# Batch 0's last slots turn their weights through VectorE and a scratch, and the last product is split into two tiles

## The chip, the cores and the metric

The kernel runs on one core of a Trainium2 chip. The metric is the device time of one execution in microseconds (us). The profile has one execution recorded by the hardware profiler; its span is the time from its first to its last instruction. All numbers are fp32.

## What is computed

Attention with a threshold for 8 batches of 8 heads, 576 rows and head size 64; then a feed-forward block with a layer norm over the 512 features, added to its own input. The reference, cut:

```python
scores = scale * np.matmul(q, k.transpose(0, 1, 3, 2))
thresh = np.max(scores, axis=-1, keepdims=True) - tau
scores = np.where(scores >= thresh, scores, -1000000000.0)
attn = np.exp(scores - np.max(scores, axis=-1, keepdims=True))
attn = attn / (np.sum(attn, axis=-1, keepdims=True) + 1e-09)
x = np.matmul(attn, v)            # heads side by side: (8, 576, 512)
...
xn = (x - mu) / np.sqrt(var + 1e-06) * g_ln
ch = np.maximum(xn @ w_ch1, 0.0) @ w_ch2     # w_ch1 512 x 2048, w_ch2 2048 x 512
return x + ch
```

The weights w_ch1 and w_ch2 arrive as 64-bit floats, and the chip converts them.

## The kernel before, in words

**Slots.** A batch is worked off in nine slots (SLOTS), numbered here n = 0, 1, ... through all batches. Slots 0 to 3 of a batch take the first 256 rows of a pair of heads, slot 4 (HP) the 64 rows left over of all pairs, and slots 5 to 8 the next 256 rows of each pair. Within a slot: TensorE makes the scores (L421) into PSUM; VectorE takes the row maxima (L435); ScalarE the exponentials into a room e (L449); VectorE masks by the threshold and sums (L456). A following slot may write its scores only when that mask has read the last ones. TensorE then multiplies the weights, turned, with v (L604, L614), one slot later.

**Two ways to turn the weights.** The product with v wants the weights transposed, in tiles em and er. Up to slot 8 (batch 0) turn_weights does it on TensorE: each block is multiplied with a diagonal matrix that holds 1/sum (L470 on ScalarE), into PSUM tiles tp and tr, and ScalarE copies these into em and er (L506, L529). From slot 9 on, turn_blocks does it: POOL divides by the sums (L472), VectorE transposes 32x32 blocks into et (L546), SyncE writes et to a scratch in DRAM (L551) and, in the next slot, fetches em and er from there (L560, L565), so that the rest of the transposition is in the addresses. by_blocks (L352) chooses. Batch 0 has its keys in another order of rows than the batches behind it (L121), so its scratch would be addressed otherwise.

**The feed-forward block.** A group is half a batch's rows (288 tokens), 16 groups in all. first_part makes the hidden layer (tile p, evicted by ScalarE, L801). Group 0 then goes through second_plain (p2, evicted at L840); the others through second_quarters, a product of quarters in seven segments of 64 matmul records each, whose sums VectorE and POOL make (L900, L908). Generators yield after each product; second_part(n, i) issues so many of these steps in each of the four quarters i of slot n that the next group is met in time. The step counts come from fixed lists (ROOM, STEPS, ready), and each engine executes its instructions in the order in which the program issues them.

**The weights' conversion.** Class Weights cuts the weights into 32 chunks of 128x512 (16 of w_ch1, 16 of w_ch2; chunk 31 is the last). A chunk is loaded from DRAM (fetch, L255, on SyncE, 512 KB), begun (two VectorE operations, L274 and L278, and two on ScalarE, L284 and L287), carried (POOL, L299), masked (VectorE, L308) and, for w_ch1, scaled (POOL, L320). Loading and conversion need room, so free lends pieces of memory that isn't in use yet: parts of w2, of hidden, of et, of x_room, of stage. fetch takes a chunk only while more than two pieces are free. BEGUN says, slot by slot, how many chunks are to be begun at three points of a slot; by slot 9 it is 32. In slots 6 to 8 six chunks a slot are begun.

**The order in a slot** (loop from L1062): scores; maxima; exponentials; quarter 0 (with the fetch of em and er, and a fetch of up to three chunks, L1077); turns of the next q and k; masks of chunks and beginning of two; quarter 1; weights (threshold, sums); masks and two more chunks; quarter 2; turn_weights or turn_blocks (L1114); a fetch of up to three chunks (L1136); masks; quarter 3; two more chunks begun. All of the loads, the scratch's write and fetch and most stores stand on SyncE's queue in this order.

**The end.** In the last group (g = 15) the last segment's product of s4 and b22 goes into one PSUM bank, is scaled by times_root (L878), added into y12, transposed (L722) and stored (L732).

Of the kernel before, what the change touches and what calls it, by code (L numbers as in the profile page):

```python
# [18 lines left out]
def kernel(  # L19
# [158 lines left out]
    class Weights:  # L178
# [13 lines left out]
        def __init__(self):  # L192
            self.chunks = [
                (w1_sb[i][:, c : c + WC], w_ch1[i * 128 : (i + 1) * 128, c : c + WC], i)
                for c in range(0, DF, WC)
                for i in range(NK)
            ] + [
                (
                    w2_sb[:, m, d : d + 4].rearrange("p d c -> p (d c)"),
                    w_ch2[d * 128 : (d + 4) * 128, m * 128 : (m + 1) * 128].rearrange(  # L200
                        "(d p) c -> p d c", p=128
                    ),
                    None,
                )
                for m in range(NK)
                for d in range(0, ND, 4)
            ]
            self.n1 = NK * (DF // WC)
            self.fetched = self.begun = self.carried = self.masked = self.scaled = 0
            self.raw, self.made, self.ticks, self.on_scalar = {}, {}, 2, []  # L210
            flat = lambda t: t.rearrange("p a b -> p (a b)")

            x_room = ffn.tile([128, NK, TOK], F32, tag="x", bufs=3, name="x_room")
            stage = self.stage = consts.tile([128, 8, WC], F32, name="stage")
            et = att.tile([128, NB, 128], F32, tag="et", bufs=1, name="et0")

            n1 = self.n1  # L220
            self.free = []
            for t, n, before in (
                (w2_sb.rearrange("p m d c -> p (m d) c"), ND // 2, lambda p: n1 + 2 * p),
                (hidden, 4, lambda p: 10),
                (et, 2, lambda p: 2 * n1),
                (x_room, 1, lambda p: 2 * n1),
                (stage, 4, lambda p: 2 * n1),
            ):
                for p in range(n):
                    self.free.append((before(p), -1, flat(t)[:, p * 2 * WC : (p + 1) * 2 * WC]))  # L230

        def piece(self, i, wait):

# [115 lines left out]
            while self.scaled < min(self.masked, self.n1):  # L349
                self.scale()  # L350

    def by_blocks(u):  # L352

        return units[u][0] > 0

    def turn(u):

        q_in, k_in = loaded.pop(u)
        qT = att.tile([128, 2, QH], F32, tag="qT", bufs=4, name="qT")
        kT = att.tile([128, S], F32, tag="kT", bufs=4, name="kT")
        ql = q_last[u % HP]
        for at in (slice(0, 8), slice(8, NB)) if u == 0 else (slice(0, NB),):
            nc.gpsimd.tensor_scalar(
                out=q_in[:, at], in0=q_in[:, at], scalar1=scl_sb, scalar2=1.0,
                op0=ALU.mult, op1=ALU.mult,  # L370
            )
        nc.vector.transpose(kT, k_in.rearrange("p n c -> p (n c)"))
        for s in range(2):
            part = q_in[:, 9 * s : 9 * s + 8]
            if by_blocks(u):
                nc.vector.transpose(
                    qT[:, s].rearrange("p (j a c) -> p a j c", j=2, a=4),
                    part.rearrange("p (a j) c -> p a j c", j=2),
                )
            else:  # L380
                nc.vector.transpose(qT[:, s], part.rearrange("p n c -> p (n c)"))
        nc.vector.transpose(
            ql.rearrange("p (t c) -> p t c", t=2),
            q_in.rearrange("p (t n) c -> p t n c", t=2)[:, :, 8],
        )
        turned[u] = (qT, kT, ql)
# [40 lines left out]
    def exponentials(n):  # L427


        neg = small.tile([128, 4], F32, tag="neg", name="neg")  # L430
        thr = small.tile([128, 4], F32, tag="thr", name="thr")
        es = e_room[(n + 1) % 2 if n < SLOTS else 0]
        for h in range(2):
            i = slice(2 * h, 2 * h + 2)
            nc.vector.tensor_reduce(  # L435
                out=neg[:, i], in_=pairs[h],
                axis=AXL.X, op=ALU.max, negate=True,
            )
            nc.gpsimd.tensor_scalar(  # L439
                out=thr[:, i], in0=neg[:, i], scalar1=-1.0, scalar2=low_sb,  # L440
                op0=ALU.mult, op1=ALU.add,
            )
            if h == 0:
                run(n, "copy")
                conversion.scale_all()
        for i in range(4):
            if i == 2:
                yield es, thr
            nc.scalar.activation(es[:, i], blocks[i], func=AF.Exp, bias=neg[:, i : i + 1])  # L449
# [82 lines left out]
            )  # L532
        yield em, er

    def turn_blocks(s, es):


        et = att.tile([128, NB, 128], F32, tag="et", bufs=1, name="et")
# [5 lines left out]
        else:  # L544
            for h in range(2):
# [2 lines left out]
                    es[:, 2 * h : 2 * h + 2].rearrange("p j (n c) -> p j n c", c=32),  # L548
                )
        scr = dram.tile([4, S, 128], F32, tag="scr", name="scr")  # L550
        nc.sync.dma_start(  # L551
            out=scr.rearrange("a (r n) x -> (a r) (n x)", r=32),
            in_=et.rearrange("p n x -> p (n x)"),
        )
        return scr

    def fetch(s, scr):

        em, er = turned_tiles(s)
        nc.sync.dma_start(  # L560
            out=em.rearrange("p a c x -> p a (c x)"),
            in_=scr[:, : J * 128].rearrange("a (p c) x -> p a (c x)", c=J),
        )
        for j in range(2):
            nc.sync.dma_start(  # L565
                out=er[64 * j : 64 * j + 64],
                in_=scr[2 * j : 2 * j + 2, J * 128 :].rearrange("a p x -> p a x"),
            )
        return em, er
# [155 lines left out]
    def send(g, m, ot):  # L725
        b, t = divmod(g, 2)
        for i in range(4):
            f = m * 128 + 32 * i
            eng = nc.sync
            if g == NG - 1:  # L730
                eng = (nc.sync, nc.gpsimd)[m % 2] if m >= HM else (nc.sync, nc.scalar)[i % 2]
            eng.dma_start(  # L732
                out=out[b, t * TOK : (t + 1) * TOK, f : f + 32].rearrange(
                    "(n r) c -> r n c", r=32
# [109 lines left out]
    def second_quarters(g, rb):  # L844
# [28 lines left out]
                at = (slice(None), slice(d, d + 4))  # L873
                eng.tensor_tensor(out=out[at], in0=in0[at], in1=in1[at], op=op)  # L874

        def times_root(out, bank):
            r = rb[:, late].unsqueeze(1).to_broadcast([128, HM, HT])
            dve.tensor_tensor(out=out, in0=bank, in1=r, op=ALU.mult)  # L878

        def segment(weights, rhs, out=None, as_it_is=False):  # L880
            bank = ps_ff.tile([128, HM, HT], F32, tag="ff", name="seg")
            for d in range(HD):
                for m in range(HM):
# [6 lines left out]
                        yield 2, 0.5  # L890
            if out is None:
                out = ffn.tile([128, HM, HT], F32, tag="part", bufs=4, name="part")
            if as_it_is:
                times_root(out, bank)
            else:
                nc.scalar.copy(out, bank)  # L896
            return out

        def add(eng, out, a, b):
            eng.tensor_tensor(out=out, in0=a, in1=b, op=ALU.add)  # L900

        def finish(eng, i, j=None):
# [6 lines left out]
            add(eng, z, z, x)  # L909

        dve, pool = nc.vector, nc.gpsimd
        done_by = pool if g < NG - 1 else dve
        later(("t3", 3, by_fours, pool, b12, b22, b12, ALU.subtract), urgent=pool)
        banks_taken[0] = True
        yield from segment(w2[0, 0], b11, y11)
# [6 lines left out]
        yield 2, 0.5  # L922
        p7 = yield from segment(s3, b12)
        yield 2, 0.5
        yield from segment(s2, b11, y21)
        need("t4")
        later(("t1", 3, by_fours, dve, b11, b22, b11, ALU.subtract), urgent=dve)
        later(
            ("u2", 1, add, pool, y21, y21, y11), ("11", 1, add, pool, y11, y11, p2),
            ("done11", 2, finish, pool, 0, 0),  # L930
        )
        yield 2, 0.5
        p4 = yield from segment(w2[1, 1], b21)
        yield 2, 0.5
        need("t1", "u2", "11")
        p5 = yield from segment(w2[1, 0], b11)
        later(
            ("u4", 1, add, dve, y12, y21, p5), ("u3", 1, add, dve, y21, y21, p7),
            ("22", 1, add, dve, y22, y21, p5), ("21", 1, add, dve, y21, y21, p4),
            ("hi", 3, finish, done_by, 1),  # L940
        )
        ends_here = g == NG - 1
        if ends_here:
            later(("done12", 2, finish, dve, 0, 1))
            later(*((f"o{m}", 1, store, dve, g, m, y[:, m]) for m in (2, 3)))
        yield 2, 0.5
        last = segment(s4, b22, as_it_is=ends_here)
        for _ in range(12):
            yield next(last)
        banks_taken[0] = False  # L950
        while waiting_mean:
            mean_of(waiting_mean.pop(0))
        p3 = yield from last
        later(("12", 1, add, dve, y12, y12, p3))
        if not ends_here:
            later(("done12", 2, finish, done_by, 0, 1))
        later(
            *((f"o{m}", 1, store, dve, g, m, y[:, m]) for m in ((2, 3, 0, 1) if g < NG - 1 else (0, 1)))
        )
        yield 2, 0.5  # L960

    def ffn_steps(g):
# [99 lines left out]
    for n in range(NS):  # L1062
# [5 lines left out]
        scores(b, s)  # L1068
        run(n, -2)
        run(n, -1)  # L1070
        rest = exponentials(n)
        es, thr = next(rest)
        run(n, 0)
# [25 lines left out]
        second_part(n, 1)  # L1099
        conversion.carry_all()  # L1100
        conversion.scale_all()
        blocks_go = by_blocks(b * HP)
        diags = weights(es, thr, blocks_go)
        run_all(aside)
        drip()
# [6 lines left out]
        conversion.carry_all()  # L1112
        box = []
        if blocks_go:  # L1114
            scr = turn_blocks(s, es)
            at_quarter(n + 1, 0, lambda s=s, scr=scr, box=box: box.append(fetch(s, scr)))
        else:

            made = turn_weights(s, es, diags)
            for i, at in enumerate(  # L1120
                (-1, -1, 0, 0) if s <= HP + 1 else (-1, -1, -1, -1) if s < 2 * HP else (-1, 0, 1, 2)
            ):
                if i < 3:
                    at_quarter(n + 1, at, next, made)
# [64 lines left out]
```

## Time and profile before

| what | us |
|---|---|
| median of 3 runs (lowest to highest) | 1357.76 (1357.47 to 1358.55) |
| the profiled execution's own time | 1357.61 |
| its span | 1355.8 |
| matmuls into tp in slots 7, 8, 9 (weights of 6, 7, 8) | 3.75, 3.75, 4.33 |
| the same into tr | 0.64, 0.64, 0.66 |
| one transpose into et (L546, 128x1152), mean | 1.374 |
| one division on POOL (L472), mean | 0.780 |
| scratch write (1152 KB), median from issue to landing | 4.9 |
| em fetch (1024 KB), the same | 5.7 |
| load of a weight chunk (512 KB), shortest, median, longest | 3.4, 4.9, 9.7 |
| last matmul's end | 1346.33 |

A line of an engine's timeline has start, length, engine, line of the kernel, operation, tile written <- tiles read, shape and count, and, in brackets, how long the engine idled before it and what it waited for. "DVE" is VectorE, "ACT" ScalarE, "PE" TensorE, "PEld" its weight loads, "SPq" SyncE's queue. Lines on matmuls often have L101, which is the helper product; there the tile tells which they are. In a table of windows a line has the window, its length, and for each engine the busy time and, in brackets, the instructions; at the end stand the clock, the DMA engines' share and GB/s.

### The profile page before, as it was taken

How to read it: one execution, taken by the hardware profiler on the slowest of the kernel's cores; microseconds unless marked ns; L12 is line 12 of the kernel's file. 1: busy time of each engine (PE TensorE's matmuls, PEld its weight loads, DVE VectorE, ACT ScalarE, POOL GpSimd, SP SyncE). 2: the span in 40 equal slices, each digit the busy share in tenths (PEclk: the TensorE clock that was granted, in tenths of full speed). 3: DMA queues.
4: the chain of work that ended last, by engine and by line, in shares of the span. 5: the costliest groups of instructions: out<-in, count | busy, mean ns of one | idle time of the engine just before them, and what ended most of it. 6: DMA issues, size and time to landing. Idle time of an engine off the chain costs nothing.

```text
span 1355.8 us, 40852 instructions
## 1 busy us (share of the span) xinstructions
PE 1326.8 (98%) x17616; PEld 1003.3 (74%) x17616; DVE 874.0 (64%) x1531; ACT 470.0 (35%) x1022; POOL 615.3 (45%) x824
## 2 busy tenths in 40 slices
PE   8999999999999999999999999999999999999997
PEld 6766657869687786968778696877869687786967
DVE  7978777666755676666766667556766667665202
ACT  4877432332423323232333323233232323333120
POOL 3554455445444344444534454443444445344312
PEclk9999999999999999999999999999999999999999
DMA  9813464457644775447744576446754376443211
GB/s 172 264 52 98 122 182 148 177 159 183 190 141 142 194 197 167 150 136 183 195 149 151 150 191 180 147 146 188 201 169 150 131 189 178 144 155 131 64 19 19
DMA packets 320996, 206.88 MB, mean 153 GB/s; under 512 B 246896, under 2 KB 278384, under 8 KB 312752
## 3 DMA queue, kind: packets, MB, share of 16 engines
q1 hardware_dynamic: 314704, 203.38, 52.0%
q8 instruction: 138, 2.26, 0.7%
q10 hardware_dynamic: 5952, 0.74, 0.4%
q0 software_dynamic: 160, 0.15, 0.1%
q14 instruction: 42, 0.34, 0.1%
HBM read 120.46 MB, written 83.76 MB: 151 GB/s over the span
## 4 chain that ended last, share of the span: by engine, by line
PE 90%; DVE 3%; ACT 2%; DMA 1%; POOL 1%; issue 1%; SPq 1%; POOLq 0%; DVEq 0%; ACTq 0%
PE p L101 37%; PE seg L101 30%; PE sc L421 10%; PE sc L604 8%; PE sc L614 2%; PE tp L101 1%; ACT e L449 1%; DVE e L456 1%; PE var L101 1%; PE mean L101 1%; SPq L118 0%; DMA x_room<-in_moe_w_ch_dram 0%; ACT em L506 0%; DMA qk_room<-in_q_dram 0%; DVE w L308 0%
## 5 line engine op out<-in xcount | busy, mean ns | idle before, releaser
L101 PE MATMUL p<-xc,w 128*64 128x288 f32 x4096 | 517.4, 408 | 6.8 <-ACT part L896 4.6
L101 PEld LDWEIGHTS p<-xc,w 128*64 128x64 f32 x4096 | 287.4, 137 | 214.4 <-issue 13.5
L435 DVE TENSOR_REDUCE neg<-sc 128x2 f32<-128x1152 f32 x144 | 188.6, 1351 | 280.8 <-PE sc L421 280.2
L472 POOL TENSOR_SCALAR e<-e,den 128x576 f32<-128x576 f32 x252 | 193.6, 780 | 133.5 <-DVE den L461 133.5
L101 PE MATMUL seg<-hidden,w 128*64 128x144 f32 x3840 | 247.9, 287 | 0.0
L101 PEld LDWEIGHTS seg<-hidden,w 128*64 128x64 f32 x3840 | 234.9, 137 | 11.5 <-issue 8.5
L456 DVE SCALAR_TENSOR_TENSOR e<-sc,thr,e 128x576 f32<-128x576 f32 x288 | 221.8, 809 | 16.9 <-POOL thr L439 11.2
L801 ACT ACTIVATE hidden<-p 128x288 f32<-128x288 f32 x256 | 106.6, 417 | 303.6 <-PE p L101 303.6
L439 POOL TENSOR_SCALAR thr<-neg,low_sb 128x2 f32<-128x2 f32 x144 | 41.4, 288 | 374.4 <-DVE neg L435 374.0
L449 ACT ACTIVATE e<-sc,neg 128x576 f32<-128x576 f32 x288 | 197.9, 755 | 2.4 <-DVE neg L435 2.4
L546 DVE STREAM_TRANSPOSE et<-e 128x1152 f32<-128x1152 f32 x112 | 153.4, 1374 | 14.7 <-POOL e L472 14.2
L421 PE MATMUL sc<-kT,qT 64*64 64x384 f32 (+3 forms) x2048 | 139.4, 403 | 3.2 <-DVE e L456 2.2
L604 PE MATMUL sc<-em,v_in 128*64 128x128 f32 (+1 forms) x2368 | 129.4, 263 | 0.0
L604 PEld LDWEIGHTS sc<-em,v_in 128*64 128x64 f32 x2368 | 122.8, 137 | 7.9
L101 PE MATMUL seg<-hidden,stage 128*64 128x144 f32 x1920 | 123.3, 286 | 0.0
L101 PEld LDWEIGHTS seg<-hidden,stage 128*64 128x64 f32 x1920 | 117.6, 137 | 2.9 <-issue 2.9
L627 ACT COPY x<-sc 128x128 f32<-128x128 f32 x120 | 31.7, 266 | 238.8 <-PE sc L421 170.4
L421 PEld LDWEIGHTS sc<-kT,qT 64*64 64x64 f32 x2048 | 76.1, 133 | 44.1 <-issue 21.2
L874 POOL TENSOR_TENSOR hidden<-hidden 128x576 f32<-128x576 f32 x60 | 84.8, 1426 | 52.1 <-ACT hidden L801 42.4
L896 ACT COPY part<-seg 128x288 f32<-128x288 f32 x74 | 29.9, 404 | 190.4 <-PE seg L101 190.0
L874 DVE TENSOR_TENSOR hidden<-hidden 128x576 f32<-128x576 f32 x60 | 51.3, 889 | 51.5 <-PE seg L101 48.5
L101 PE MATMUL seg<-hidden,e 128*64 128x144 f32 x960 | 65.3, 286 | 0.0
(145 smaller groups left out, 1098.9 us busy)
## 6 DMA issues: line engine op xcount, KB each, us to landing
scr<-et SPq DMA_DIRECT2D x63, 1152.0 KB, 4.9
em<-scr SPq DMA_DIRECT2D x63, 1024.0 KB, 5.7
q_in<-in_q_dram SPq DMA_DIRECT2D x124, 72.0 KB, 2.7
out_dram<-ot SPq DMA_DIRECT2D x248, 36.0 KB, 3.8
k_in<-in_k_dram SPq DMA_DIRECT2D x120, 72.0 KB, 3.0
er<-scr SPq DMA_DIRECT2D x126, 64.0 KB, 5.2
v_in<-in_v_dram SPq DMA_DIRECT2D x28, 256.0 KB, 5.5
w<-in_moe_w_ch_dram SPq DMA_DIRECT2D x12, 512.0 KB, 4.8
```

The source lines that it names most:

```text
L101: nc.tensor.matmul(out[r], lhsT=lhsT[:, r], rhs=rhs, **flags)
L421: nc.tensor.matmul(sc[h][64 * i : 64 * i + 64, at : at + n], lhsT=ql[r] if s == HP else qT[r, half, j * 128 + 64 * i : j * 128 + 64 * i + 64],
L435: nc.vector.tensor_reduce(out=neg[:, i], in_=pairs[h], axis=AXL.X, op=ALU.max, negate=True,)
L439: nc.gpsimd.tensor_scalar(out=thr[:, i], in0=neg[:, i], scalar1=-1.0, scalar2=low_sb, op0=ALU.mult, op1=ALU.add,)
L449: nc.scalar.activation(es[:, i], blocks[i], func=AF.Exp, bias=neg[:, i : i + 1])
L456: nc.vector.scalar_tensor_tensor(out=es[:, i], in0=blocks[i], scalar=thr[:, i : i + 1], in1=es[:, i], op0=ALU.is_ge, op1=ALU.mult, accum_o ...
L472: nc.gpsimd.tensor_scalar(out=es[:, i], in0=es[:, i], scalar1=den[:, i : i + 1], scalar2=1.0, op0=ALU.mult, op1=ALU.mult,)
L546: nc.vector.transpose(et[:, :, 64 * h : 64 * h + 64].rearrange("p n (j c) -> p j n c", j=2), es[:, 2 * h : 2 * h + 2].rearrange("p j (n c) ...
L604: nc.tensor.matmul(dst[64 * h : 64 * h + 64], lhsT=vt[:, h, c, :], rhs=pick(em[:, 2 * j : 2 * j + 2, c], h), start=c == 0 and first, stop= ...
L627: nc.scalar.copy(x_of(2 * b + (s > HP))[:, s % (HP + 1), 128 * j : 128 * j + 128], pv[j])
L801: nc.scalar.activation(hidden[:, d], p1, func=AF.Relu)
L874: eng.tensor_tensor(out=out[at], in0=in0[at], in1=in1[at], op=op)
```

## The change

- by_blocks now asks for the slot and not the batch: from FIRST = HP + 2 = 6 on the weights are turned by blocks. So slots 6, 7 and 8 change, all of batch 0. Its scratch is written in four DMAs and em fetched in four, with rows of 512 bytes.
- et is no longer lent as two pieces to the conversion. In its place the room e[1] is lent (take) from slot 7 on, when its weights (slot 6) are turned; so the exponentials from slot 7 on go into e[0].
- In second_quarters the sums u3 and 21 are made after the fifth product and not after the sixth, with other tiles of y as room; in the last group row 21 is finished there as well, then 22 and 12 behind the sixth.
- In the last group the last product is made by last_tiles as two PSUM tiles, one for each block of 128 features. Each is scaled, added, transposed and sent by itself; what is waiting is issued before the first one.

```diff
-            et = att.tile([128, NB, 128], F32, tag="et", bufs=1, name="et0")
...
-                (et, 2, lambda p: 2 * n1),
...
+        def take(self, t):
+            t = t.rearrange("p a b -> p (a b)")
+            for p in range(2):
+                self.free.append((2 * self.n1, -1, t[:, p * 2 * WC : (p + 1) * 2 * WC]))
...
-    def by_blocks(u):
-        return units[u][0] > 0
+    FIRST = HP + 2
+    def by_blocks(n):
+        return n >= FIRST
...
-            if by_blocks(u):
+            if by_blocks(units[u][0] * SLOTS + units[u][1] + (HP + 1 if s else 0)):
...
-        es = e_room[(n + 1) % 2 if n < SLOTS else 0]
+        es = e_room[(n + 1) % 2 if n <= FIRST else 0]
...
-    def turn_blocks(s, es):
+    def turn_blocks(b, s, es):
...
+        if b == 0:
+            for a in range(4):
+                nc.sync.dma_start(
+                    out=scr[a].rearrange("(n r) x -> r n x", r=32), in_=et[32 * a : 32 * a + 32]
+                )
+            return scr
...
+        for a in range(0 if b else 4):
+            nc.sync.dma_start(
+                out=em[:, a], in_=scr[a, : J * 128].rearrange("(c p) x -> p c x", p=128)
+            )
...
-                eng = (nc.sync, nc.gpsimd)[m % 2] if m >= HM else (nc.sync, nc.scalar)[i % 2]
+                eng = ((nc.sync, nc.scalar), (nc.sync, nc.scalar), (nc.sync,), (nc.gpsimd,))[m]
+                eng = eng[i % len(eng)]
...
+        def last_tiles(weights, rhs):
+            for m in range(HM):
+                bank = ps_ff.tile([128, HT], F32, tag="ff", name="end")
+                for d in range(HD):
+                    product(
+                        bank, lhsT=weights[:, m, d], rhs=rhs[:, d],
+                        start=d == 0, stop=d == HD - 1,
+                    )
+                    if d < HD - 1:
+                        yield 2, 0.5
+                drip(everything=True)
+                z = ffn.tile([128, HT], F32, tag="part", bufs=4, name="z")
+                dve.tensor_tensor(out=z, in0=bank, in1=rb[:, late], op=ALU.mult)
+                add(dve, y12[:, m], y12[:, m], z)
+                store(dve, g, m, y[:, m])
+                run_all(stores)
+                if m < HM - 1:
+                    yield 2, 0.5
...
+        later(("u3", 1, add, dve, y22, y12, p7), ("21", 1, add, dve, y21, y22, p4))
+        if ends_here:
+            later(("done21", 2, finish, dve, 1, 0))
...
+        later(("22", 1, add, dve, y22, y22, p5), ("u4", 1, add, dve, y12, y12, p5))
         if ends_here:
+            later(
+                ("done22", 2, finish, dve, 1, 1), ("done12", 2, finish, dve, 0, 1),
+                *((f"o{m}", 1, store, dve, g, m, y[:, m]) for m in (2, 3)),
+            )
+        else:
+            later(("hi", 3, finish, pool, 1))
...
+        last = last_tiles(s4, b22) if ends_here else segment(s4, b22)
...
+        if n == FIRST + 1:
+            conversion.take(e_room[1])
...
-        blocks_go = by_blocks(b * HP)
+        blocks_go = by_blocks(n)
...
-                (-1, -1, 0, 0) if s <= HP + 1 else (-1, -1, -1, -1) if s < 2 * HP else (-1, 0, 1, 2)
+                (-1, -1, 0, 0)
```

More of the change, by code (lines that the diff above doesn't have):

```diff
@@ L555, in turn_blocks, with fetch @@
         return scr
-    def fetch(s, scr):
+    def fetch(b, s, scr):
         em, er = turned_tiles(s)
[L560 to L563, printed above, removed]
+        for a in range(0 if b else 4):
+            nc.sync.dma_start(
+                out=em[:, a], in_=scr[a, : J * 128].rearrange("(c p) x -> p c x", p=128)
+            )
+        if b:
+            nc.sync.dma_start(
+                out=em.rearrange("p a c x -> p a (c x)"),
+                in_=scr[:, : J * 128].rearrange("a (p c) x -> p a (c x)", c=J),
+            )
         for j in range(2):
@@ L874, in by_fours, with segment @@
                 eng.tensor_tensor(out=out[at], in0=in0[at], in1=in1[at], op=op)
[L876 to L880, printed above, removed]
+        def segment(weights, rhs, out=None):
             bank = ps_ff.tile([128, HM, HT], F32, tag="ff", name="seg")
@@ L892, in segment @@
                 out = ffn.tile([128, HM, HT], F32, tag="part", bufs=4, name="part")
[L893 to L896, printed above, removed]
-            return out
+            nc.scalar.copy(out, bank)
+            return out
+        def last_tiles(weights, rhs):
[16 more added lines that the diff above has]
+                    yield 2, 0.5
         def add(eng, out, a, b):
@@ L911, in second_quarters @@
         dve, pool = nc.vector, nc.gpsimd
-        done_by = pool if g < NG - 1 else dve
+        ends_here = g == NG - 1
         later(("t3", 3, by_fours, pool, b12, b22, b12, ALU.subtract), urgent=pool)
@@ L924, in second_quarters @@
         yield 2, 0.5
-        yield from segment(s2, b11, y21)
+        yield from segment(s2, b11, y12)
         need("t4")
@@ L928, in second_quarters @@
         later(
-            ("u2", 1, add, pool, y21, y21, y11), ("11", 1, add, pool, y11, y11, p2),
+            ("u2", 1, add, pool, y12, y12, y11), ("11", 1, add, pool, y11, y11, p2),
             ("done11", 2, finish, pool, 0, 0),
@@ L936, in second_quarters @@
         p5 = yield from segment(w2[1, 0], b11)
[L937 to L942, printed above, removed]
-        if ends_here:
-            later(("done12", 2, finish, dve, 0, 1))
-            later(*((f"o{m}", 1, store, dve, g, m, y[:, m]) for m in (2, 3)))
+        later(("22", 1, add, dve, y22, y22, p5), ("u4", 1, add, dve, y12, y12, p5))
+        if ends_here:
+            later(
+                ("done22", 2, finish, dve, 1, 1), ("done12", 2, finish, dve, 0, 1),
+                *((f"o{m}", 1, store, dve, g, m, y[:, m]) for m in (2, 3)),
+            )
+        else:
+            later(("hi", 3, finish, pool, 1))
         yield 2, 0.5
-        last = segment(s4, b22, as_it_is=ends_here)
+        last = last_tiles(s4, b22) if ends_here else segment(s4, b22)
         for _ in range(12):
@@ L953, in second_quarters @@
         p3 = yield from last
-        later(("12", 1, add, dve, y12, y12, p3))
         if not ends_here:
[L956 to L959, printed above, removed]
+            later(
+                ("12", 1, add, dve, y12, y12, p3), ("done12", 2, finish, pool, 0, 1),
+                *((f"o{m}", 1, store, dve, g, m, y[:, m]) for m in (2, 3, 0, 1)),
+            )
         yield 2, 0.5
@@ L1114 @@
         if blocks_go:
-            scr = turn_blocks(s, es)
-            at_quarter(n + 1, 0, lambda s=s, scr=scr, box=box: box.append(fetch(s, scr)))
+            scr = turn_blocks(b, s, es)
+            at_quarter(n + 1, 0, lambda b=b, s=s, scr=scr, box=box: box.append(fetch(b, s, scr)))
         else:
```

## The prediction

> **What bounds the kernel now.** I read the page first: its busy lines name TensorE.
>
> ```profile
> PE 1326.8 (98%) x17616; PEld 1003.3 (74%) x17616; DVE 874.0 (64%) x1531; ACT 470.0 (35%) x1022; POOL 615.3 (45%) x824
> ```
>
> That is a mean over unlike stages. Slots 6, 7 and 8 (counted from 0) lie where the feed-forward weights are still being converted, so I took the busy time by slot; a slot runs from one scores matmul (L421) to the next: slot 7, 8, 9, then 11.
>
> ```profile
> 100.54:122.51 21.97, 21.00 (x252) 14.28 (x248) 19.02 (x30) 16.99 (x37) 11.64 (x12) 1.00 0.45 136
> 122.51:145.23 22.72, 22.50 (x269) 15.18 (x264) 19.59 (x35) 16.82 (x34) 10.83 (x12) 1.00 0.44 110
> 145.23:170.24 25.01, 22.87 (x269) 15.14 (x264) 18.78 (x32) 8.30 (x17) 10.92 (x13) 1.00 0.37 87
> ...
> 189.14:205.73 16.59, 16.57 (x180) 10.09 (x176) 12.67 (x23) 6.71 (x16) 9.62 (x12) 1.00 0.68 174
> ```
>
> After the length come PE, PEld, DVE. In slot 11 PE is busy throughout and DVE has 3.9 us to spare. In slots 7 and 8 DVE has 19.0 of 22.0 and 19.6 of 22.7: here both are full. Which ends last is seen in the VectorE timeline:
>
> ```profile
> 103.29 2.61 DVE L435 TENSOR_REDUCE neg<-sc 128x2 f32<-128x1152 f32 x2
> ...
> 122.96 0.69 DVE L308 SCALAR_TENSOR_TENSOR w<-w 128x512 f32<-128x512 f32 x1 [1.19 <-POOL w L299]
> ...
> 126.68 2.61 DVE L435 TENSOR_REDUCE neg<-sc 128x2 f32<-128x1152 f32 x2
> ...
> 149.93 2.58 DVE L435 TENSOR_REDUCE neg<-sc 128x2 f32<-128x1152 f32 x2
> ...
> 162.07 2.82 DVE L546 STREAM_TRANSPOSE et<-e 128x1152 f32<-128x1152 f32 x2 [0.56 <-POOL e L472]
> 164.81 0.44 DVE L722 STREAM_TRANSPOSE ot<-o 128x288 f32<-128x288 f32 x1
> 171.94 0.43 DVE L274 TENSOR_SCALAR stage<-x_room 128x512 uint32<-128x512 uint32 x1 [6.70 <-DMA x_room<-in_moe_w_ch_dram]
> ```
>
> The reductions of slots 7, 8 and 9 have no idle time before them: their scores were ready, and they waited for VectorE's conversions of the slot before. So this is a VectorE chain. Slot 9 already goes by VectorE and scratch, and shows the price: after the transposes VectorE stands 6.70 us for weight chunk 31 (the last 512 KB). SyncE's timeline says why, and TensorE's who pays:
>
> ```profile
> 164.91 0.36 SPq L551 DMA_DIRECT2D scr<-et  x1
> 165.37 0.40 SPq L255 DMA_DIRECT2D x_room<-in_moe_w_ch_dram  x1
> ```
>
> ```profile
> 179.22 2.16 PE L101 MATMUL p<-hidden,w 128*64 128x288 f32 x16 [1.37 <-DVE w L308]
> ```
>
> SyncE issues in order: the chunk's load stood behind the scratch write, which stood for the transposes, and it landed 7.0 us after the write's issue. TensorE came to the matmul of chunk 31 at 177.84 and waited for its mask (L308, 178.51). **This is the gate**: what TensorE saves before it is worth nothing unless that mask comes earlier; what the mask loses, the end loses.
>
> **The change, part by part.**
>
> *Removed from TensorE.* For each of the slots the matmuls into tp (64 records) and tr (8). Rows, in the slot after: 3.75, 3.75 and 4.33 us of tp for slots 6, 7 and 8, and 0.64, 0.64, 0.66 of tr: 13.8 us. ScalarE loses 4 diag products (1.26 us), 4 copies of 0.59 and one of 0.37 a slot. All before the gate; by itself worth nothing.
>
> *Added on VectorE.* Two transposes a slot, 1.37 us each (L546): 2.8. POOL gets four divisions of 0.78 us a slot (L472). They run while VectorE converts two chunks before its transposes (2.2 us at least, after the last reciprocal); the bounds are nothing (an added operation cannot shorten) and 1 us a slot, what a VectorE operation of 0.69 us loses where it meets POOL (L278 took 1.67 to 1.77 in five places), and I take nothing.
>
> *The planner.* et no longer lends its two pieces; the second exponentials' room lends two from slot 7. Followed through the free list, every chunk begins, is carried and masked at the same quarter as now, so the steps of the products keep their places. The loads are issued for chunk 23 (and 24, 25) after slot 7's transposes and for 28 and 29 after slot 8's, as now in the program. But now SyncE meets no wait there and runs ahead: chunk 23 was issued at 102.84 for use at 124.64, chunks 28 and 29 from 137.69 for use at 146.40 and 147.46. With a scratch write ahead of them that waits for the transposes, they are issued when the transposes end, as chunk 31 is now. Behind the write on SyncE stand these loads and v; in slot n+1 the em fetch waits for the write to land, and behind it stand chunks 21 and 22 (in slot 7), 26 and 27 (8), and 30 (9).
>
> *Step by step, by the start of the reduction.* In batch 0 the write is four DMAs; at 0.36 us of issue each that is 3 x 0.36 = 1.1 us more than the one of slot 9. So a load behind it lands 7.0 + 1.1 = 8.1 us after the transposes end. No row has this write in 512-byte packets. Bounds: 5.5 (issued 0.6 after, landed in 4.9, the median of all weight loads) and 11.3 (issued 1.6 after, landed in 9.7, the longest of them). I take 8.1, since chunk 31 is nearest: the same bytes on the same queue.
> 1. Slot 7's reduction: 2.8 more, less the 1.18 us that VectorE waits at 99.47 for POOL: **+1.6** (1 to 2.8).
> 2. Slot 8's: now from 121.10, where the transposes will stand, to 126.68 is 5.6 us (two masks, 1.19 of waiting, chunks 22 and 23). Then: 2.8, the load at 8.1, chunk 23's two operations 1.1: 12.0. **+6.4**.
> 3. Slot 9's: from 141.84 to 149.93 is 8.1 us. Then: 2.8; chunk 28 landed at 8.1 and 29 some 1.6 later (estimated: 512 KB at 323 GB/s, the rate in the window from 167 to 168 us); 1.1 of work on it and 0.46 for the transpose of a store (L722): 14.1. **+6.0**.
> 4. Chunk 30 stands behind the em fetch: the write lands after some 7, six issues take 2.7, landing 7.5 (5.7 of em and some 1.8 for the chunk): 17.2 after the transposes; it is wanted 17.0 after them (the 11.3 to the reduction and the 5.7 from 149.93 to 155.61). **+0.5** (0 to 2), for what the sums leave open.
> The mask of chunk 31 is then 1.6 + 6.4 + 6.0 + 0.5 = 14.5 us late: 178.5 becomes 193. TensorE, 13.8 us lighter, stands for VectorE for some 28 us between 100 and 193.
>
> Weighed against the Trainium skill, page "DMA: Bandwidth & Descriptors", section "Anatomy of one DMA — SWDGE (gpsimd) path", measured there for POOL's DMAs: 2.0 us and bytes over 436 GB/s, which would land a 512 KB chunk 3.2 us after its issue; the trace's chunk 31 took 6.6, behind 1152 KB. By the rule each of the two waits would be 3.4 us shorter and the time 1363.8; I go by the row, which has the same bytes ahead.
>
> *After the gate* slots are TensorE's (16.57 of 16.59 us in slot 11), in the same order, with nothing to catch up in: 14.5 us stay.
>
> *The other orderings.* Room e, the other layout of q's turn (L376 for L381, 0.38 us each either way) and the sums u3 and 21 one segment earlier are the same instructions; VectorE at 64% hides them; within 0.5 us to either side. em lands some 14 us after the transposes and is read in the last quarter of the next slot, later than that.
>
> *The last group.* The tail now:
>
> ```profile
> 1342.96 1.93 DVE L900 TENSOR_TENSOR y<-y,part 128x288 f32<-128x288 f32 x4 [7.49 <-ACT part L896]
> ...
> 1347.26 0.83 DVE L722 STREAM_TRANSPOSE ot<-y 128x288 f32<-128x288 f32 x2
> 1347.76 5.46 SPq L732 DMA_DIRECT2D out_dram<-ot  x8
> 1348.01 0.42 DVE L878 TENSOR_TENSOR part<-seg,rb 128x288 f32<-128x288 f32 x1
> ```
>
> The last matmul ends at 1346.33, but VectorE reaches its sum at 1348.01. Afterwards two sums (0.97) and the finish of 21 (a half of 1.52) are done before, in the 7.49 us that VectorE idles; left from 1342.96 are 2 sums (0.97), two finishes (1.8) and two transposes (0.83): 1346.55 and not 1348.09, **1.5 us** earlier, and the stores with it. The two halves need 0.25 + 0.25 + 0.42 each: the second ends near 1348.5 and not 1349.85. The stores keep their queues (the table in send gives each the one it had) and their order on them, so all move by 1.5 us (0.5, if the last wait of SyncE for an earlier store, 1.8 us, keeps its place, to 2).
>
> Sum on the profiled execution (1357.61 us, span 1355.8; the median of the runs is 0.15 higher): 1357.6 + 14.5 - 1.5 = **1370.6 us**.
>
> **Rivals.**
> A, *no wait for loads*: VectorE only gets longer. 1.6, then 2.8 less 1.2 of present waits twice: +4.8, less 1.5: 1360.9; up to 1365 with half of the waits. For it: loads in other slots were early. Against: the order on SyncE.
> B, *faster*: the matmuls, copies and diag products feed VectorE's present waits. The chain of waits goes through tp and em at 124.63 to 128.36, on to POOL and qT. Place: VectorE's idle time from 100.5 to 178.5, 13.9 us with the 6.70 (the rest are 1.95, 1.19, 1.23, 1.21, 0.44, 0.56 and 0.66). If all went: 8.4 - 13.9 - 1.5 = -7.0: 1350.6. It decides when more than 8.4 us of them go and no new one comes; 7.2 remain without the load's, so the 6.70 must shrink too.
> C, *gain and loss cancel*: VectorE loses 4 of its idle time and pays the 8.4: +4.4 - 1.5 = 1360.5, and a little more recovered is within 0.2% (1354.9 to 1360.3; about what a measurement of this kernel can tell from no change).
> D, *dearer*: loads land at 11.3 in both slots: two times 3.2 more: 1377.0. For it: 512-byte packets and more in the queue (v behind slot 7's). Against: chunk 31 had v behind it too.
>
> **Chances.** Forecast (1365 to 1374) 0.58; A 0.17; D 0.08; B 0.11; C 0.06. So faster 0.11, same 0.06, slower 0.83. The range reaches over A to the upper half of D: 1360.5 to 1376.
>
> **What would show it.** Right: in slots 7 and 8 VectorE stands 4 to 6 us each for a load of a weight chunk, with scr issued just before it; the wait at chunk 31 stays near 6.7; TensorE stands for VectorE's masks and for ScalarE in slots 7 to 10, and slot 10's reduction begins near 188. Wrong: chunks 23, 28 and 29 issued before the transposes end, or a mask of chunk 31 at or before 178.5.

## The result, and the profile after

| | before | after |
|---|---|---|
| median of the runs, us | 1358.12 (4 runs, 1357.47 to 1358.55) | 1381.82 (4 runs, 1380.29 to 1383.44) |
| ratio to before, 95% interval | | 1.0172 (1.0160 to 1.0184) |
| the profiled execution, its span | 1357.61, 1355.8 | 1380.29, 1378.5 |

The change makes the kernel 23.7 us slower by the medians, 22.7 by the two profiled executions, which the following compares. The forecast was 1370.6: the sign is right, the size is not, and the time lies above the range (1360.5 to 1376). In the page after, TensorE's busy time has hardly fallen, though 216 matmul records are gone (13.8 us in the rows before), and the clock row has dips where it was 9 throughout before:

```profile
PE 1325.7 (96%) x17400; PEld 997.1 (72%) x17400; DVE 880.6 (64%) x1544; ACT 458.8 (33%) x995; POOL 626.8 (45%) x836
...
PEclk9999879999999999999999999999999999999999
```

VectorE's timeline after, with the lines that answer to those of before (line numbers have moved: L435 is L440):

```profile
106.33 2.61 DVE L440 TENSOR_REDUCE neg<-sc 128x2 f32<-128x1152 f32 x2
...
138.08 0.43 DVE L277 TENSOR_SCALAR stage<-w 128x512 uint32<-128x512 uint32 x1 [8.63 <-DMA w<-in_moe_w_ch_dram]
...
139.15 2.62 DVE L440 TENSOR_REDUCE neg<-sc 128x2 f32<-128x1152 f32 x2
...
170.00 0.43 DVE L277 TENSOR_SCALAR x_room<-e 128x512 uint32<-128x512 uint32 x1 [8.64 <-DMA e<-in_moe_w_ch_dram]
...
174.01 2.59 DVE L440 TENSOR_REDUCE neg<-sc 128x2 f32<-128x1152 f32 x2
...
194.87 0.43 DVE L277 TENSOR_SCALAR e<-stage 128x512 uint32<-128x512 uint32 x1 [6.69 <-DMA stage<-in_moe_w_ch_dram]
...
201.44 0.65 DVE L311 SCALAR_TENSOR_TENSOR w<-e 128x512 f32<-128x512 f32 x1
```

The last line is the mask of chunk 31. Before, it was:

```profile
178.51 0.65 DVE L308 SCALAR_TENSOR_TENSOR w<-stage 128x512 f32<-128x512 f32 x1
```

Chunks 23, 28 and 31 are what VectorE stands for: 8.63 and 8.64 us where it stood for nothing, and 6.69 as before (6.70). The reductions of slots 7, 8 and 9 are 3.0, 12.5 and 24.1 us later, chunk 31's mask 22.9 (201.44, it was 178.51). SyncE's timeline has the loads behind the scratch's write, and the write's four issues at 3.8 us together:

```profile
127.23 3.82 SPq L558 DMA_DIRECT2D scr<-et  x4
131.16 1.42 SPq L258 DMA_DIRECT2D w<-in_moe_w_ch_dram  x1
...
159.25 3.83 SPq L558 DMA_DIRECT2D scr<-et  x4
```

TensorE, slots 8 and 9 and the gate:

```profile
142.43 11.31 PE L101 MATMUL p<-hidden,w 128*64 128x288 f32 x68 [13.12 <-ACT hidden L818]
...
182.44 0.70 PE L620 MATMUL sc<-em,v_in 128*64 128x128 f32 x4 [10.42 <-DVE e L461]
...
199.28 1.15 PE L101 MATMUL mean<-sum,avg_sb 128*64 128x288 f32 x4 [2.21 <-POOL sum L672]
...
202.14 4.11 PE L101 MATMUL p<-hidden,w 128*64 128x288 f32 x16 [0.75 <-DVE w L311]
```

It stands where it was busy, and when it works again it is slow: the 68 records take 11.31 us, the 16 behind the gate 4.11. Before, the 16 took 2.16 and the 68 took 8.42:

```profile
132.93 8.42 PE L101 MATMUL p<-hidden,w 128*64 128x288 f32 x68
```

The windows after, at the gate (after the five engines the granted clock, the DMA share and GB/s):

```profile
200.00:202.00 2.00, 1.39 (x6) 0.24 (x2) 1.74 (x5) 0.50 (x1) 0.23 (x1) 0.50 0.02 4
202.00:204.00 2.00, 1.86 (x8) 1.01 (x10) 2.00 (x6) 0.00 (x0) 0.00 (x0) 0.50 0.69 114
204.00:206.00 2.00, 2.00 (x10) 0.95 (x8) 1.97 (x8) 0.00 (x0) 0.67 (x1) 0.50 0.67 106
```

From the gate to the end the difference is kept, but for two terms: these 2.0 us of half clock, and the tail, which takes 7.2 us from the last matmul's end (1371.31) in place of 9.5. 22.9 + 2.0 - 2.3 = 22.6 of the 22.7 us.

### The profile page after: what moved, and what is told of

Its sections match the earlier page's. It is cut to its first block, busy times and chain, and to the rows that moved or that the text cites. A ratio compares the mean times of both kernels' runs of the same rounds, so it can differ in the third digit from the quotient of the medians.

```text
span 1378.5 us, 40484 instructions
## 1 busy us (share of the span) xinstructions
PE 1325.7 (96%) x17400; PEld 997.1 (72%) x17400; DVE 880.6 (64%) x1544; ACT 458.8 (33%) x995; POOL 626.8 (45%) x836
## 4 chain that ended last, share of the span: by engine, by line
PE 88%; DVE 4%; DMA 3%; ACT 2%; SPq 2%; issue 1%; POOL 1%; POOLq 0%; ACTq 0%; DVEq 0%
PE p L101 36%; PE seg L101 30%; PE sc L426 9%; PE sc L620 8%; PE sc L630 2%; PE tp L101 1%; ACT e L454 1%; SPq L118 1%; DVE et L551 1%; DVE e L461 1%; PE var L101 1%; SPq L558 1%; DMA w<-in_moe_w_ch_dram 1%; PE mean L101 0%; DMA stage<-in_moe_w_ch_dram 0%
## 5 line engine op out<-in xcount | busy, mean ns | idle before, releaser
L440 DVE TENSOR_REDUCE neg<-sc 128x2 f32<-128x1152 f32 x144 | 188.7, 1352 | 280.5 <-PE sc L426 280.5
L477 POOL TENSOR_SCALAR e<-e,den 128x576 f32<-128x576 f32 x264 | 205.7, 791 | 134.6 <-DVE den L466 134.6
L551 DVE STREAM_TRANSPOSE et<-e 128x1152 f32<-128x1152 f32 x118 | 161.4, 1374 | 14.4 <-POOL e L477 13.8
L620 PE MATMUL sc<-em,v_in 128*64 128x128 f32 (+1 forms) x2368 | 131.4, 265 | 11.3 <-DVE e L461 11.3
L827 POOL TENSOR_TENSOR hidden<-hidden 128x288 f32<-128x288 f32 x48 | 38.9, 811 | 54.6 <-ACT hidden L825 52.1
```

The source lines that it names most:

```text
L440: nc.vector.tensor_reduce(out=neg[:, i], in_=pairs[h], axis=AXL.X, op=ALU.max, negate=True,)
L477: nc.gpsimd.tensor_scalar(out=es[:, i], in0=es[:, i], scalar1=den[:, i : i + 1], scalar2=1.0, op0=ALU.mult, op1=ALU.mult,)
L551: nc.vector.transpose(et[:, :, 64 * h : 64 * h + 64].rearrange("p n (j c) -> p j n c", j=2), es[:, 2 * h : 2 * h + 2].rearrange("p j (n c) ...
L620: nc.tensor.matmul(dst[64 * h : 64 * h + 64], lhsT=vt[:, h, c, :], rhs=pick(em[:, 2 * j : 2 * j + 2, c], h), start=c == 0 and first, stop= ...
L827: nc.gpsimd.tensor_tensor(out=sq[:, 0], in0=sq[:, 0], in1=sq[:, c], op=ALU.add)
```

## The experiments

Each is compared with the kernel before on the same chip. Two theories stood against each other: **queue**, that VectorE stands for loads that SyncE can't issue before the scratch write; and **VectorE**, that its own added work lengthens the chain, and the loads' waits only fill what would be lost anyway.

### e1_tail_only and e2_blocks_only: the two parts alone

```diff
# e1: the changed kernel without the blocks
+            et = att.tile([128, NB, 128], F32, tag="et", bufs=1, name="et0")
...
+                (et, 2, lambda p: 2 * n1),
...
-    FIRST = HP + 2
+    FIRST = SLOTS
...
-        if n == FIRST + 1:
-            conversion.take(e_room[1])
...
-                (-1, -1, 0, 0)
+                (-1, -1, 0, 0) if s <= HP + 1 else (-1, -1, -1, -1) if s < 2 * HP else (-1, 0, 1, 2)
# e2: the changed kernel with second_quarters and send of before
```

> The kernel before with the change's last group alone (last_tiles, the moved sums); weights of slots 6 to 8 stay on TensorE. If the two parts of the change are independent, the profile after gives the price of this part: from the last matmul's end to the end of the span 7.2 us in place of 9.5, so 2.3 us less: 1355.8 us. Rival: the tail is bound by the drain of the stores, and the moved sums cost POOL or VectorE something in the 14 groups before: 1357 to 1359 us.

> The change's other part alone: slots 6 to 8 through VectorE and scratch, with the last group as before. If the parts add: 1381.8 + 2.3 = 1384 us, chunk 31's mask again near 201. Rival, that the last group's reordering has a share in the loss: below 1382 us.

Measured: e1 1355.82 us (0.9989, interval 0.9980 to 0.9998), e2 1382.28 (1.0181, 1.0167 to 1.0195). The whole loss is the blocks'. The last group's part is a gain, but these runs don't give its size: it is 2.4 us by e1's medians and 1.5 by its ratio, whose interval reaches from 0.3 to 2.7; the medians of e2 and after lie only 0.5 apart, their spans (1380.4 and 1378.5) 1.9.

### e3_ahead: the loads ahead of the scratch

```diff
+        if n > HP + 2:
+            conversion.fetch(3)
         run(n, 0)
...
+        if n >= HP + 2:
+            conversion.fetch(3)
         if blocks_go:
             scr = turn_blocks(b, s, es)
```

(and the same calls taken out behind them)

> The changed kernel with every load of a weight chunk from slot 6 on issued ahead of the scratch's write and of the em fetch of the same slot; nothing else is moved. Theory queue (VectorE stands for loads that are held behind the scratch write on SyncE): the waits of 8.6, 8.6 + 0.7 and 6.7 us go, chunk 31's mask comes at about 178 in place of 201.4, and the end with it: 1355 to 1358 us. Rival VectorE (its transposes and POOL's divisions stretch the chain by themselves, and another wait takes the place of the loads'): mask at 185 to 192, 1365 to 1373 us. Rival transfers (the DMA engines are full, so the loads land late in any order): waits of 5 us and more stay, over 1373 us.

Measured: 1361.68 us (1.0023, 1.0013 to 1.0033), 20.1 below the changed kernel with the same instructions on every engine. VectorE's waits for chunks 23, 28 and 29 are gone; 0.75 us for chunk 30 and one long wait, for chunk 31, are left:

```profile
131.93 2.61 DVE L440 TENSOR_REDUCE neg<-sc 128x2 f32<-128x1152 f32 x2
...
157.61 2.58 DVE L440 TENSOR_REDUCE neg<-sc 128x2 f32<-128x1152 f32 x2
...
177.38 0.43 DVE L277 TENSOR_SCALAR e<-stage 128x512 uint32<-128x512 uint32 x1 [4.75 <-DMA stage<-in_moe_w_ch_dram]
```

The time lies between the expectations of queue and VectorE, and so does chunk 31's mask (183.9): the queue theory holds for most of the loss, but not for all. Between the reductions of slots 8 and 9 there are now 25.7 us where the kernel before has 23.25, with no wait for a load; VectorE is busy in 24.95 of them, before in 20.57. That is its own work. Chunk 31's load was issued only at 172.69, behind q, k and the stores on SyncE.

### e4_long_rows and e5_four_long: what made the write dear

```diff
# e4: one DMA each way, as in the later batches
-        if b == 0:
+        if False:
             for a in range(4):
...
# e5: four DMAs, long rows
-                    out=scr[a].rearrange("(n r) x -> r n x", r=32), in_=et[32 * a : 32 * a + 32]
+                    out=scr[a].rearrange("(r n) x -> r n x", r=32), in_=et[32 * a : 32 * a + 32]
```

> The changed kernel with batch 0's scratch written and fetched as in the later batches: one DMA of 9 KB rows, and one fetch of 2 KB rows, in place of four DMAs each of 512-byte rows. The weights of slots 6 to 8 then meet the wrong keys; only the time is read. The prediction had a load land 8.1 us after the transposes, and it took 10.8. If the four DMAs of short rows on SyncE are what was mis-sized: loads land 7 us after the transposes, 3.8 earlier in two slots, 7 to 8 us in all: 1374 us. If the loads are late for the amount of bytes ahead of them: within 2 us of 1382.

> The changed kernel with batch 0's scratch still written and fetched by four DMAs each, but in long rows (9 KB written, 2 KB fetched) in place of 512 bytes; the weights of slots 6 to 8 meet the wrong keys, only the time is read. With one DMA of long rows the time was 1373.2, with four of 512 bytes 1381.8. If the number of DMAs is what cost the 8.6 us: at least 1379 us, and the write's issue on SyncE takes 3 to 4 us again. If the short rows are: 1373 to 1376 us, the four issues take 1.4 us together, as the prediction had it.

Measured: e4 1373.19 us (1.0111, 1.0095 to 1.0126), e5 1377.79 (1.0145, 1.0131 to 1.0158). In SyncE's and VectorE's timelines, e4 first, then e5:

```profile
127.22 0.34 SPq L562 DMA_DIRECT2D scr<-et  x1
127.67 0.38 SPq L258 DMA_DIRECT2D w<-in_moe_w_ch_dram  x1
```

```profile
134.43 0.43 DVE L277 TENSOR_SCALAR stage<-w 128x512 uint32<-128x512 uint32 x1 [4.99 <-DMA w<-in_moe_w_ch_dram]
```

```profile
126.90 3.06 SPq L558 DMA_DIRECT2D scr<-et  x4
130.07 1.28 SPq L258 DMA_DIRECT2D w<-in_moe_w_ch_dram  x1
```

```profile
136.04 0.43 DVE L277 TENSOR_SCALAR stage<-w 128x512 uint32<-128x512 uint32 x1 [6.92 <-DMA w<-in_moe_w_ch_dram]
```

From the write's issue to VectorE's first operation on chunk 23 it takes 7.2 us behind one DMA of long rows (the 7.0 of slot 9, which the prediction used), 9.1 behind four DMAs of long rows, 10.85 behind four of 512-byte rows. e5 falls between its two expectations: the number of DMAs and the length of the rows each cost about half, 1.9 and 1.7 us a load. The four issues don't take 4 x 0.36 us in either case: 3.06 here, 3.82 there, for as many bytes. In the profile after the first of the four takes 0.33 us and the last 1.64:

```profile
127.23 0.33 SPq L558 DMA_DIRECT2D scr<-et  x1
...
129.41 1.64 SPq L558 DMA_DIRECT2D scr<-et  x1
```

### e6_warm: TensorE kept busy ahead of the gate

```diff
+        for _ in range(14 if g == 1 else 0):
+            product(means[g][:, :128], lhsT=avg_sb, rhs=ident, start=True, stop=True)
         product(means[g], lhsT=avg_sb, rhs=sums.pop(g), start=True, stop=True)
```

> The changed kernel with 14 idle products (128 columns, about 0.24 us each, results overwritten) on TensorE ahead of the mean of group 1, where TensorE stands before the matmul of chunk 31. In the profile after the granted clock is 0.50 from 200 to 206 us and the 16 matmul records behind the gate take 4.11 us; before they took 2.16. Theory clock (the idle time costs some 2 us behind the gate by itself): 1379.8 us, the 16 records near 2.2. Rival (they are slow for another reason): 1381.8 or more.

Measured: 1379.14 us (1.0156, 1.0142 to 1.0170), 2.7 below the changed kernel (2.2 by the two ratios). The idle products and the 16 records:

```profile
198.21 3.23 PE L101 MATMUL mean<-ident,avg_sb 128*64 128x128 f32 x56
...
203.70 2.16 PE L101 MATMUL p<-hidden,w 128*64 128x288 f32 x16 [1.29 <-DVE w L311]
```

The granted clock is 1.00 in every microsecond from 198 to 210. So the slow records are the clock's, and TensorE's idleness costs twice here: once in itself and once behind it.

### e7_ahead_early, e10_ahead_long: what is left when no load is late

```diff
# e7: e3, and chunk 31 at the start of slot 9
-        def fetch(self, most=99):
+        def fetch(self, most=99, wait=1):
...
-                got = self.piece(i, 1)
+                got = self.piece(i, wait)
...
-            conversion.fetch(3)
+            conversion.fetch(3, 0 if n == SLOTS else 1)
# e10: e7 with the scratch of e4
```

> As e3_ahead, and chunk 31's load issued with chunk 30's at the start of slot 9, ahead of the em fetch and of the q and k loads. In e3 VectorE still stood 4.75 us for chunk 31, because its load came late on SyncE's queue. Theory queue: that wait goes too, chunk 31's mask comes at about 179 in place of 183.9: 1356 to 1358 us. What is then left over the kernel with the new last group alone (1355.8) is VectorE's own work. Rival: the wait moves to another chunk, 1360 to 1362 us.

> e7_ahead_early with batch 0's scratch written and fetched by one DMA each of long rows (the weights of slots 6 to 8 meet the wrong keys; only the time is read). In e7 TensorE stands 4.7 us for em of slot 8, then 0.9 for slot 9's threshold. Theory (the short rows' DMAs delay em): em comes 6 us earlier, TensorE then waits for slot 9's threshold on VectorE alone: 1357 to 1359 us, still above e8's 1354.65 by VectorE's own work. Rival (VectorE is the bound already): 1360 or more.

Measured: e7 1360.74 us (1.0019, 1.0009 to 1.0028), e10 1359.21 (1.0008, 0.9999 to 1.0018). In e7 VectorE waits for loads only 0.93 and 0.40 us, and TensorE for no chunk's mask; the time is hardly better than e3's, as the rival had it, but the wait has moved to another place than a chunk. TensorE in e7, then in e10:

```profile
169.40 0.70 PE L620 MATMUL sc<-em,v_in 128*64 128x128 f32 x4 [4.68 <-DMA out_dram<-ot]
```

```profile
168.41 0.69 PE L620 MATMUL sc<-em,v_in 128*64 128x128 f32 x4 [4.43 <-DVE e L461]
```

In both, the product of slot 8's weights with v stands 4.4 to 4.7 us. The releaser named in e7 is a store's DMA, and e10's expectation took the wait for one for em. VectorE's timeline, in e7 and then in e10, says otherwise:

```profile
169.22 0.09 DVE L461 DVE_READ_ACCUMULATOR e<-sc,thr,e 128x1 f32 x1
```

```profile
168.23 0.08 DVE L461 DVE_READ_ACCUMULATOR e<-sc,thr,e 128x1 f32 x1
```

This ends the first half of slot 9's threshold, which reads the PSUM tile (sc) that the product writes: at 169.31 in e7 and 168.31 in e10. TensorE starts 0.1 us behind it both times, as in the profile after (182.34 and 182.44). Those two of em's four DMAs that the first matmuls read had been issued by 161.2 in e7 and took at most 6.3 us, so they had landed by 167.5. The wait is VectorE's chain in both. e10 is 1.5 us faster by the medians, with intervals that overlap; in its trace the waits of 0.93 and 0.40 us are gone and the threshold ends 1.0 us earlier.

### e8_tail_ahead_early: the version that beats both

```diff
# e1 with the fetches of e3 and e7; slots 6 to 8 on TensorE
```

> The kernel before with the new last group and all loads of weight chunks ahead of the scratch and the em fetch, chunk 31's with chunk 30's in slot 9; weights of slots 6 to 8 stay on TensorE. If the gate is read rightly, VectorE's 6.7 us of waiting in slot 9 go, and TensorE loses only its own wait of 1.4 us at chunk 31, being the bound then: 1355.8 - 1.4 = 1354.4 us. Rival (the time follows VectorE): 1349 to 1351 us. Rival (early loads only compete): 1355.8 or more.

Measured: 1354.65 us (0.9978, 0.9969 to 0.9987). The gain over e1 is 1.2 by the medians (1.5 by the ratios, whose intervals overlap): about TensorE's wait of 1.4 at the gate, and no more, though VectorE no longer stands 6.7 us for chunk 31. TensorE's wait at the gate is gone from the trace (the 4 records before it and the 16 behind it are one row), and slot 10's reduction now waits for TensorE:

```profile
177.65 2.60 PE L101 MATMUL p<-hidden,w 128*64 128x288 f32 x20
```

```profile
172.85 2.62 DVE L442 TENSOR_REDUCE neg<-sc 128x2 f32<-128x1152 f32 x2 [2.39 <-PE sc L428]
```

### e9_slot8_early: a smaller dose

```diff
-        return n >= FIRST
+        return n >= FIRST + 2
```

(and the fetches of e7; the turning of slots 6 and 7 is spread over the next slot as before)

> As e7_ahead_early (all loads of chunks ahead), but only slot 8's weights go by VectorE and scratch; those of slots 6 and 7 stay on TensorE. It tells whether a smaller dose pays. TensorE loses 5 us of matmuls and 2 us of waits in slot 9; against it em of slot 8 comes 17.6 us after the transposes' end (as in e7), near 164.5, and slot 9's threshold ends near 166, where the kernel with none of it (e8) reads em at 166.6. Theory (em's way and VectorE's chain are now the bound): 1353.5 to 1356 us, no gain over e8's 1354.65. Rival (the matmuls' time is won): 1348 to 1351 us.

Measured: 1356.13 us (0.9992, 0.9983 to 1.0000). No gain over e8, a small loss if any: TensorE stands 4.38 us for the same product (164.75), after one slot by blocks as after three. Here too the first half of slot 9's threshold ends 0.1 us before that start, at 164.64. So the wait is VectorE's chain and not em's way, which the expectation named beside it.

## Why the prediction was wrong

**The gate** (right). Chunk 31's mask decided; TensorE's 13.8 us were worth nothing. e8 shows it from the other side: with the loads early, TensorE gains just its own wait there.

**The loads held on SyncE** (right in kind). They came at the chunks that were named, 23, 28, 29; e3 takes 20.1 us off by their order alone. The waits were named at 4 to 6 us each and were 8.63 and 8.64.

**The step that failed** is the size of one term: "at 0.36 us of issue each that is 3 x 0.36 = 1.1 us more than the one of slot 9. So a load behind it lands 7.0 + 1.1 = 8.1 us after the transposes end". It was 10.85 and 10.75 (e4, e5: 3.6 us dearer than one DMA, and not 1.1). The prediction took the issue time of one large DMA, 0.36 us, for that of each of four in a row; they took 3.8 together, and the load behind them 1.4 to 1.6 to issue and not 0.4. The forecast had this inside its bounds (11.3), and its rival D at 11.3 gave 1377.0, but the chance was put on the near end.

With 10.85 and 10.75 in place of 8.1 the sum would have been 5.4 us higher, 1376.0, the upper end of the range. The rest of the 9.7 us that are missing on the profiled execution is in smaller terms: 3.0 in slot 9's reduction, 1.4 in slot 7's, 0.3 in slot 8's and 2.0 of clock, less 1.6 at chunk 30 and 0.8 at the tail.

**Slot 9's reduction** was mis-sized a second time: +11.6 us from slot 8's and not +6.0. Landing has 2.7 of it. From slot 8's reduction to the end of its transposes the profile after has 20.1 us (139.15 to 159.2) where the prediction had 15.2 + 2.8 = 18.0: four operations of the conversion run longer (L277 0.89; L281 1.11, 1.69 and 1.70; alone they take 0.42 and 0.69). By POOL's timeline two of them, 0.9 us, meet its divisions:

```profile
151.54 2.54 POOL L477 TENSOR_SCALAR e<-e,den 128x576 f32<-128x576 f32 x2 [0.18 <-DVE den L466]
154.75 1.37 POOL L302 TENSOR_TENSOR w<-w,stage 128x512 int32<-128x512 int32 x1 [0.68 <-ACT stage L287]
```

The other two, 2.0 us, meet carries (L302), which the new order of things put beside them. The value taken for POOL's company was nothing, with 1 us as the bound. The last 0.9 us are chunk 29's: it came 1.8 us behind chunk 28 and not 1.6, and its first operation took 1.14 us.

**Slot 7's reduction** +3.0 and not +1.6, of which 0.8 were there by slot 5's (66.86, it was 66.05), ahead of anything that the blocks change; traces with the same instructions up to there lie between 66.4 and 67.4, so that this part is scatter. **Chunk 30**: +0.5 forecast; it came in time, and the step from slot 9's to slot 10's reduction is 22.3 and was 23.45.

**After the gate** "14.5 us stay" left out the clock: 2.0 us in the profile (e6: 2.2 to 2.7).

**The tail** was right in kind, and in size as far as this can be told: 1.5 us were forecast. From the last matmul's end to the end of the span the ten traces with the new last group take 7.1 to 7.9 us, the two with the old one 9.1 and 9.5; the pair compared above, 2.3 us apart, is near the upper end. In the profile after, the two halves' transposes come 1.05 apart and the second is begun 1.8 us after the last matmul's end, where it was 3.1:

```profile
1372.03 0.48 DVE L738 STREAM_TRANSPOSE ot<-y 128x288 f32<-128x288 f32 x1 [0.32 <-DVE y L931]
...
1373.08 0.48 DVE L738 STREAM_TRANSPOSE ot<-y 128x288 f32<-128x288 f32 x1
```

**The rivals.** e3 and e7, at 1361.7 and 1360.7, come near to the forecast for A (no waits for loads), 1360.9, but partly by luck: e3 still has 4.75 us of such a wait, and in e7 the end is set by slot 9's threshold and not by chunk 31's mask, on which A's sum rests. It wasn't the change's case. B (VectorE recovers its idle time) isn't seen in any run.

What stays open: in e7 and e10, 4.6 to 6.1 us above e8, how much is VectorE's transposes, how much POOL's company, and how much TensorE's clock; why the later issues of four take longer than the first was not tested either.

## What to carry to other kernels

Before work is taken off the busiest engine, look for what that engine meets next that it can't pass, and ask whether that comes earlier too. A DMA that waits for an engine holds all that stands behind it on its queue, as the scratch's write did on SyncE's: list those and put what has nothing to wait for ahead (here 20 us by order alone). The price of a split transfer wasn't the number of its pieces times the issue of one (3.8 us for four, one alone 0.36): measure the issue of several in a row.

## What the hardware showed that was not expected

- Four DMAs in a row on SyncE's queue took 3.06 to 3.48 us to issue (32 rows of 9 KB each; e5) and 3.81 to 3.83 (576 rows of 512 bytes each; the profile after), where one of the same total took 0.34 to 0.36 (e4). The load behind the four short-rowed ones then took 1.4 to 1.6 us to issue, behind one DMA 0.38 to 0.46. The Trainium skill, page "DMA: Bandwidth & Descriptors", section "Issuing engines are not separate DMA queues", has the sequencer's time to initiate a DMA as usually small against the DMA; here the four issues are 3.8 us together, against 3.1 to 5.6 us from the issue of each to its landing.
- TensorE's granted clock was 0.50 from 200 to 206 us, behind a wait of 2.21 us (the row of 199.28), at 2.0 us of loss; with 14 idle products in the gap it stayed at 1.00 (e6). The skill, page "TensorE: Matmul & The Clock Gate", section "What's actually happening", has the fall after an idle window of about 3.4 us; here the matmul behind 2.21 us of idleness, with busy time before and behind it, was already slow (1.15 us for 4 records that take 0.66). The length of one wait doesn't settle it: in e4 the same 4 records behind 3.28 us of idleness took 0.71, and the clock fell only after them (0.50 from 194 to 200 us).
